# A gated linear attention feeding a PReLU network: first score products issued earlier, half-block products paired, later loads without the zero rows

## The chip, the cores and the metric

The kernel runs on one core of one Trainium2 chip. A core has a matrix engine (PE, with its weight loads shown apart as PEld), a vector engine (DVE), a scalar engine (ACT), a general engine (POOL), an engine that only issues transfers (SP), and 16 DMA engines that all queues share. Each engine works through its own instructions in order. The metric is the device time in microseconds (us); lower is better.

## The reference

Two stages are computed in float32. The first is a recurrence over 768 time steps for 4 batches and 8 heads of width 48; the second is a two-layer network with a PReLU between its layers.

```python
def _attn_ref(q, k, v, f_logit):          # (4, 8, 768, 48)
    f = 1.0 / (1.0 + np.exp(-f_logit))
    state = np.zeros((B, H, D, D))
    for t in range(S):
        state = f[:, :, t, :, None] * state + np.einsum('bhd,bhe->bhde', k[:, :, t], v[:, :, t])
        y[:, :, t] = np.einsum('bhd,bhde->bhe', q[:, :, t], state)
def _moe_ref(x, w_in, w_out, alpha):      # x: (3072, 384), d_ff 2048
    h = x @ w_in
    g = np.maximum(h, 0.0) + alpha * np.minimum(h, 0.0)
    return g @ w_out
```

## The kernel before

**Steps.** The sequence is cut into chunks of 128 time steps, and two batches (`U = 2`) are taken together, which gives 12 steps. The first two steps are the first chunk (`c == 0`) of either pair of batches; the very first one is `bp == 0, c == 0`. A step has four parts, each a generator that is advanced by the letters of a schedule string: `prepare` (letters P and Q), `carry` (O), `attend` (S) and `network` (n). While the network of one step runs, the attention of the next step and the preparation of the one after it are woven in. The order on PE, DVE and ACT is exactly the order of these letters (four strings in `first`, then `usual`); SP and POOL get their order from the framework, which also places the waits.

**Attention.** Within a chunk the scores are built from blocks of 32 (`DB`), 16 and 4 time steps. `prepare` loads `f`, `q`, `k` laid out as 128 rows (two heads of 48 rows, each followed by 16 rows of zeros), takes the sigmoid of `f` on ACT, and forms running products of `f` on DVE. From these come scaled copies of `q` and `k`: `qd` (short distances), `k4` and `us`, `k16` and `q16` (the later half of a block of 32 against its earlier half, for the first chunk only), `kh` and `q3`, `ks`. In `attend`, PE makes the products `raw` (L518: `k` times `qd`) and `qu` (L533: `k4` times `us`) for `u = 0` and then `u = 1`; DVE picks entries of them into `ad` by copies under a mask (L524, L555). ACT copies `ad` into the score matrix `A` (L561), PE multiplies it by the values (`py`, L572), ACT copies `py` to `y` (L581). In `carry`, PE makes `off` (L442 from `kh` and `q3`; L452 from `k16` and `q16`), the transposes `pk` (L469) and the state update `pd` (L482); ACT copies them out (L456 to `ad`, L460 to `A`, L472 to `ksn`, L498 to `vs`).

**Network.** For the first step `xt` (L590) turns `y` into `xT` on PE; later steps do it by DMA. Then 8 groups of `ph` (L614, 12 recorded matmuls each) with a ReLU on ACT (L619) and a combination on DVE (L622), and `po` (L638).

**Weights.** `w_in` and `w_out` each come in 8 pieces. A piece is loaded by SP into one of 4 `raw` buffers; two ACT passes (L197, L199) and three DVE passes (L205, L211, L218) decode it; POOL issues a DMA that adds its last part (L225; for the very first piece DVE adds it, L223). Letters a and b are the ACT halves for `w_in` and `w_out`, w and v the DVE halves. A `w_in` piece holds just what one `ph` group needs.

**PSUM.** `psa` has two buffers of two banks ("pair"), taken in turn by `off`, `pk`, `raw`, `qu`, `pd`, `py`; `psn` has four single banks ("bank") for `xt`, `ph`, `po`. `qd`, `ad` and `A` exist once, and so do the loaded `f`, `q`, `k`.

**Loads.** For the first step SP issues `f`, `q`, `k` and `v`; for all later steps POOL does, in its own order among the weight additions (L264, L274).

Of the kernel before, what the change touches and what calls it, by code (L numbers as in the profile page):

```python
# [8 lines left out]
F32 = mybir.dt.float32  # L9
# [22 lines left out]
def kernel(  # L32
# [63 lines left out]
    def bank(name):  # L96
        return psn.tile([128, 512], F32, tag="net", name=name)

    om = const.tile([128, NF], F32, tag="om", name="om")
    w_in_sb = const.tile([128, NK, DF], F32, tag="w_in", name="w_in_sb")  # L100
    w_out_sb = const.tile([128, NF, DM], F32, tag="w_out", name="w_out_sb")
# [43 lines left out]


    A = const.tile([128, U, H, C], F32, tag="A", name="A")
    nc.gpsimd.memset(A, 0.0)
    vs = []
    for bp in range(B // U):  # L150
# [105 lines left out]
    def prepare(bp, c, x):  # L256
# [2 lines left out]
        b0 = U * bp  # L259
        loads = nc.gpsimd if bp or c else nc.sync  # L260

        def load(name, src, bufs=2):
            t = work.tile([128, W], F32, tag=name, name=f"{name}_{i}", bufs=bufs)
            loads.dma_start(out=t.rearrange("p (u x) -> p u x", u=U),  # L264
                              in_=src[b0:b0 + U, c].rearrange("u p h t -> p u (h t)"))
            return t

        f = quads(load("f", fT, 1))
        q = load("q", qT, 1)
        k = x["k"] = load("k", kT, 1)  # L270

        for cc in range(NC2):
            t_, _ = halves(cc)
            loads.dma_start(out=vs[bp][t_, cc, :, 0:DM], in_=v[b0:b0 + U, c, t_].rearrange("u t d -> t u d"))  # L274


        nc.scalar.activation(f, f, AF.Sigmoid)
        nc.scalar.copy(kr[:, :, 2:3], f[:, :, 3:4])
        qdv = [qd[:, :, QO[d]:QO[d] + NB * (4 - d)].rearrange("p g (i r) -> p g i r", r=4 - d) for d in range(4)]
        nc.scalar.copy(qd[:, :, 0:DB], q.rearrange("p (g t) -> p g t", t=DB))  # L280
# [11 lines left out]
        nc.vector.tensor_tensor(fq, f[:, :, 0:1].rearrange(by32, i=NB), kr[:, :, 0:1].rearrange(by32, i=NB), ALU.mult)  # L292
        lagged(3)
        yield

# [129 lines left out]
                        in_=kt[32 * a:32 * (a + 1), 0:W].rearrange("p (g b x) -> p g b x", b=NJ, x=32)[:, :, b, 0:n])  # L427
        yield

    def carry(bp, c, x):  # L430

        i = f"{bp}_{c}"
        q3, ks, kh, f64 = (x[n] for n in ("q3", "ks", "kh", "f64"))
        off = pair(f"off_{i}")
        for u in range(U):
            for hp in range(HP):
                for cc in range(NC2):
                    g = (u * HP + hp) * NC2 + cc
                    o = (u * HP + hp) * DB
                    for par in range(2):  # L440
                        r_ = rows(par)
                        nc.tensor.matmul(off[CH * cc:CH * cc + DB, par, o:o + DB],  # L442
                                         lhsT=kh[r_, g], rhs=q3[r_, g, 2], start=True, stop=True)
        if not c:
            for u in range(U):
                for hp in range(HP):
                    for j in range(NJ):
                        g = (u * HP + hp) * NJ + j
                        o = U * HP * DB + (u * HP + hp) * 16
                        for par in range(2):  # L450
                            r_ = rows(par)
                            nc.tensor.matmul(off[DB * j:DB * (j + 1), par, o:o + 16], lhsT=x["k16"][r_, g],  # L452
                                             rhs=x["q16"][r_, g], start=True, stop=True)
            for u in range(U):
                o = U * HP * DB + u * HP * 16
                nc.scalar.copy(ad[:, u, :, :, 16:DB], off[:, :, o:o + HP * 16].rearrange("p r (h t) -> p r h t", h=HP))  # L456
        for cc in range(NC2):
            s_ = slice(CH * cc, CH * cc + DB)
            for par in range(2):
                nc.scalar.copy(A[s_, :, par * HP:(par + 1) * HP, CH * cc + DB:CH * (cc + 1)],  # L460
                               off[s_, par, 0:U * HP * DB].rearrange("p (u h t) -> p u h t", u=U, h=HP))


        if not c:
            pk = pair(f"pk_{i}")
            for u in range(U):
                for hp in range(HP):
                    a = (u * HP + hp) * NC2
                    nc.tensor.transpose(pk[:, u, hp * 128:(hp + 1) * 128], ks[:, a:a + 2].rearrange("p c s t -> p (c s t)"), ident)  # L469
            ksn = x["ksn"] = work.tile([128, U, HP * 128], F32, tag="ksn", name=f"ksn_{i}", bufs=1)  # L470
            for u in range(U):
                nc.scalar.copy(ksn[:, u], pk[:, u])  # L472
        yield
        pd = pair(f"pd_{i}")
        ksn = x["ksn"]
        for u in range(U):
            for hp in range(HP):
                for cc in range(NC2):
                    for par in range(2):
                        o = (u * HP + hp) * D  # L480
                        s_ = halves(cc)[0]
                        nc.tensor.matmul(pd[rows(par), cc, o:o + D],  # L482
                                         lhsT=ksn[s_, u, hp * 128 + 64 * par:hp * 128 + 64 * par + D],
                                         rhs=vs[bp][s_, cc, u, (2 * hp + par) * D:(2 * hp + par + 1) * D], start=True, stop=True)

        def moved(cc):

            of, to = halves(cc)[1], halves(1 - cc)[1]
            was, then = (vs[bp][p, a, :, 0:DM].rearrange("p u (h e) -> p u h e", e=D)
                         for p, a in ((of, cc), (to, 1 - cc)))  # L490
            if c or cc:
                nc.vector.tensor_tensor(then, was, f64[of].unsqueeze(3).broadcast_to((D, U, H, D)), ALU.mult)
            for par in range(2):
                now = pd[rows(par), cc, 0:U * HP * D].rearrange("p (u h e) -> p u h e", u=U, e=D)
                if c or cc:
                    nc.vector.tensor_tensor(then[:, :, par:H:2], then[:, :, par:H:2], now, ALU.add)
                else:
                    nc.scalar.copy(then[:, :, par:H:2], now)  # L498

        x["moved"] = moved  # L500
        moved(0)
        yield

    def attend(bp, c, x):

        i = f"{bp}_{c}"
        k, k4, us = (x[n] for n in ("k", "k4", "us"))


        QL, QS = (UW, UW) if c else (VW, C)  # L510
        for u in range(U):
            raw = pair(f"raw{u}_{i}")
            for hp in range(HP):
                for j in range(NJ):
                    g = (u * HP + hp) * NJ + j
                    for par in range(2):
                        r_ = rows(par)
                        nc.tensor.matmul(raw[DB * j:DB * (j + 1), par, hp * C:hp * C + QW],  # L518
                                         lhsT=k[r_, g * DB:(g + 1) * DB], rhs=qd[r_, g], start=True, stop=True)
            adu = ad[:, u].rearrange("p r h (i t) -> p (r h) i t", t=4)  # L520
            rv = raw.rearrange("p r (h x) -> p (r h) x", h=HP)
            for d in range(4):
# [5 lines left out]
            for hp in range(HP):  # L528
                for j in range(NJ):
                    g = (u * HP + hp) * NJ + j  # L530
                    for par in range(2):
                        r_ = rows(par)
                        nc.tensor.matmul(qu[DB * j:DB * (j + 1), par, hp * QS + 4:hp * QS + QL],  # L533
                                         lhsT=k4[r_, g * DB:(g + 1) * DB], rhs=us[r_, g, 4:QL], start=True, stop=True)
            if c:
                for m in range(1, NB):
                    lo = UO[m] + (4 if m == 1 else 0)
                    n = DB - 4 * m
                    nc.vector.copy_predicated(  # L539
                        ad[:, u, :, :, 4 * m:DB],  # L540
                        mquad[:, lo:lo + n].bitcast(I32).unsqueeze(1).unsqueeze(1).broadcast_to((128, 2, HP, n)),
                        qu[:, :, 0:HP * UW].rearrange("p r (h x) -> p r h x", h=HP)[:, :, :, lo:lo + n])
            else:
                qv = qu.rearrange("p r (h x) -> p (r h) x", h=HP)
                adh = ad[:, u].rearrange("p r h (a t) -> p (r h) a t", a=2)
                for m in range(1, NQ):
                    n = 4 * (NQ - m)
                    lo = 4 if m == 1 else VO[m]
                    hi = lo + (DB - 4 if m == 1 else 2 * n)
                    to, of, by = ad[:, u].rearrange("p r h t -> p (r h) t")[:, :, 4:DB], qv[:, :, lo:hi], mhalf[:, lo:hi]  # L550
                    by = by.bitcast(I32).unsqueeze(1).broadcast_to((128, H, hi - lo))
                    if m > 1:
                        to = adh[:, :, :, 4 * m:16]
                        of, by = (t.rearrange("p h (a t) -> p h a t", a=2) for t in (of, by))
                    nc.vector.copy_predicated(to, by, of)  # L555
            yield

        for u in range(U):
            for j in range(NJ):
# [46 lines left out]
    def network(bp, c, x):  # L606
# [44 lines left out]

    steps = [(bp, c) for c in range(NC) for bp in range(B // U)]
    first = (
        "P2 a P w P a P a w O P w S a w S Q a O a w S2 Q w S Q S",
        "P a w a P w2 b n2 v O n b2 v S n v n P S b S v b n S v n b v Q b n b n v O v n v Q3 S2 n2 Q2",
        "O n2 S n2 S Q S2 n3 O n Q n Q2 n S2 n Q2 n",
        "n O n2 S n2 S Q n O Q n2 S Q n S n S Q2 S Q n2",
    )
    usual = "O n S n2 S n2 O n Q n Q2 n2 S3 n Q S n Q n Q"
    pieces = {key: part for keys, parts in (("aw", load_weights(w_in_sb, w_in, "w_in")),  # L660
# [75 lines left out]
```

## Time and profile before

| quantity | us |
|---|---|
| time, median of 8 runs (lowest, highest) | 653.5 (651.24, 654.11) |
| the profiled execution's own time | 650.54 |
| its span in the trace | 648.8 |
| PE busy (7580 matmuls) | 608.4, 94% |
| DVE busy | 423.8, 65% |
| ACT busy | 254.9, 39% |
| POOL busy | 67.6, 10% |

The page gives for each engine its busy time and, in 40 equal slices of 16.2 us, the busy share of each slice in tenths. The chain of work that ended last is followed back from the last instruction; "issue" in it is time for which the profile shows no wait. The timeline merges equal instructions that follow one another: start, length from the first to the last, engine, source line, operation, output and inputs, count, and in brackets the idle time before the first with what ended it. Line numbers are those of the kernel before.

### The profile page before, as it was taken

What the parts mean: (1) busy time and instruction counts of PE and PEld (TensorE: products, weight loads), DVE (VectorE), ACT (ScalarE), POOL (GpSimd) and SP (SyncE); (2) the same over time, 40 slices, a digit from 0 to 9 for tenths busy, and PEclk for the clock granted to TensorE, in tenths of its full rate; (3) what the DMA queues carried; (4) which work ended last, traced back from release to release, by engine and by line L of the source; (5) the groups of instructions that cost most, each with busy time, mean ns of one, the idle gap of its engine ahead of it and who ended that gap; (6) DMA issues with size and microseconds to landing.
All of it is one profiled execution on the core that took longest, in us unless ns stands there. A gap on an engine that the chain in (4) does not pass through costs nothing.

```text
span 648.8 us, 17589 instructions
## 1 busy us (share of the span) xinstructions
PE 608.4 (94%) x7580; PEld 451.5 (70%) x7580; DVE 423.8 (65%) x866; ACT 254.9 (39%) x466; POOL 67.6 (10%) x114
## 2 busy tenths in 40 slices
PE   0449799999999999999999999999999999999997
PEld 0448666866866876876875876876876776786874
DVE  6879798794695785685686686587577476450220
ACT  5676783423343161361361360460361351331210
POOL 9143221000000010010000000000001000000000
PEclk9999899999999999999999999999999999999999
DMA  7998985413223223223213313313213201101000
GB/s 250 279 244 224 288 223 128 112 34 61 59 79 63 70 67 63 69 55 73 72 40 87 74 33 91 74 34 90 68 41 90 52 27 35 42 1 25 24 1 24
DMA packets 73116, 56.22 MB, mean 87 GB/s; under 512 B 47408, under 2 KB 64944, under 8 KB 73040
## 3 DMA queue, kind: packets, MB, share of 16 engines
q0 software_dynamic: 10112, 27.53, 16.0%
q1 hardware_dynamic: 57536, 25.37, 15.4%
q10 hardware_dynamic: 5392, 2.21, 1.6%
q8 instruction: 60, 0.98, 0.6%
q14 instruction: 16, 0.13, 0.1%
HBM read 36.21 MB, written 4.72 MB: 63 GB/s over the span
## 4 chain that ended last, share of the span: by engine, by line
PE 93%; DVE 2%; issue 2%; ACT 2%; DMA 1%; DVEq 0%; ACTq 0%
PE ph L614 40%; PE po L638 39%; PE raw L518 3%; PE py L572 3%; PE qu L533 3%; PE pd L482 2%; PE off L442 1%; PE xt L590 1%; DMA f<-in_fT 1%; ACT A L561 0%; PE pk L469 0%; PE off L452 0%; ACT us L312 0%; DVE ad L524 0%; DVE us L319 0%
## 5 line engine op out<-in xcount | busy, mean ns | idle before, releaser
L614 PE MATMUL ph<-xT,w_in_sb 128*128 128x256 f32 x1152 | 262.2, 385 | 2.6 <-issue 2.6
L638 PE MATMUL po<-w_out_sb,g 128*128 128x384 f32 x768 | 252.9, 488 | 0.0
L614 PEld LDWEIGHTS ph<-xT,w_in_sb 128*128 128x128 f32 x1152 | 216.5, 191 | 35.7 <-issue 6.2
L638 PEld LDWEIGHTS po<-w_out_sb,g 128*128 128x128 f32 x768 | 144.9, 190 | 96.8
L622 DVE SCALAR_TENSOR_TENSOR g<-neg,om,ph 128x256 f32<-128x256 f32 x192 | 83.3, 477 | 163.3 <-ACT neg L619 163.2
L619 ACT ACTIVATE neg<-ph 128x512 f32<-128x512 f32 x96 | 57.4, 601 | 166.3 <-PE ph L614 156.7
L632 ACT COPY o<-po 128x384 f32<-128x384 f32 x24 | 11.5, 478 | 145.6 <-PE po L638 131.7
L524 DVE COPY_PREDICATED ad<-mraw,raw 128x256 f32<-128x256 int32 (+1 forms) x96 | 42.4, 441 | 5.8 <-PE raw L518 3.3
L539 DVE COPY_PREDICATED ad<-mquad,qu 128x224 f32<-128x224 int32 (+6 forms) x140 | 41.9, 299 | 6.2
L561 ACT COPY A<-ad 32x256 f32<-32x256 f32 x96 | 38.4, 400 | 2.2 <-DVE ad L539 0.9
L328 DVE TENSOR_TENSOR us<-us,fs 128x768 f32<-128x768 f32 (+5 forms) x60 | 37.2, 620 | 0.3
L312 ACT COPY us<-qd 128x256 f32<-128x256 f32 x48 | 30.2, 666 | 9.8 <-DVE qd L285 9.7
L264 POOL DMA_DIRECT2D k<-in_kT x11 | 8.3, 759 | 233.8 <-PE raw L518 207.1
L285 DVE TENSOR_TENSOR qd<-qd,f 128x768 f32<-128x768 f32 (+2 forms) x36 | 27.2, 755 | 8.1 <-ACT qd L280 8.0
L572 PEld LDWEIGHTS py<-A,vs 128*64 128x64 f32 x768 | 25.0, 145 | 10.3 <-ACT A L561 8.1
L415 ACT COPY A<-q 48x512 f32<-48x512 f32 x44 | 27.1, 616 | 9.3 <-DVE f L410 4.6
L572 PE MATMUL py<-A,vs 128*64 128x64 f32 x768 | 26.9, 231 | 3.9 <-ACT A L561 3.9
L518 PE MATMUL raw<-qd,k 48*32 48x80 f32 x1536 | 23.8, 243 | 6.6 <-issue 5.2
L518 PEld LDWEIGHTS raw<-qd,k 48*32 48x32 f32 x1536 | 18.7, 109 | 15.0 <-issue 14.3
L442 PE MATMUL off<-q,kh 48*32 48x32 f32 x768 | 9.5, 199 | 18.4 <-DVE q L366 18.4
L581 ACT COPY y<-py 128x512 f32<-128x512 f32 x24 | 12.9, 589 | 35.2 <-PE py L572 35.2
L533 PE MATMUL qu<-us,k 48*32 48x112 f32 (+1 forms) x1536 | 25.5, 259 | 0.0
(85 smaller groups left out, 441.0 us busy)
## 6 DMA issues: line engine op xcount, KB each, us to landing
w_out_raw<-in_w_out SPq DMA_DIRECT2D x8, 767.8 KB, 6.6
w_in_raw<-in_w_in SPq DMA_DIRECT2D x8, 767.2 KB, 7.1
f<-in_fT POOLq DMA_DIRECT2D x11, 512.0 KB, 4.0
q<-in_qT POOLq DMA_DIRECT2D x11, 512.0 KB, 4.1
k<-in_kT POOLq DMA_DIRECT2D x11, 512.0 KB, 4.3
out<-o SPq DMA_DIRECT2D x24, 192.0 KB, 2.1
vs<-in_v POOLq DMA_DIRECT2D x22, 192.0 KB, 3.5
w_out_sb<-w_out_lead POOLq DMA_DIRECT2D x8, 384.0 KB, 5.2
```

The lines of the kernel that those rows point to most:

```text
L312: nc.scalar.copy(q4[:, :, :, r], qdv[r][:, :, :, 0])
L328: nc.vector.tensor_tensor(us[:, :, UO[m]:UO[m] + 4 * n].rearrange("p g (i r) -> p g i r", r=4), us[:, :, skip:skip + 4 * n].rearrange("p g ...
L518: nc.tensor.matmul(raw[DB * j:DB * (j + 1), par, hp * C:hp * C + QW], lhsT=k[r_, g * DB:(g + 1) * DB], rhs=qd[r_, g], start=True, stop=True)
L524: nc.vector.copy_predicated(adu[:, :, :, d:4], mraw[:, d, :, d:4].bitcast(I32).unsqueeze(1).broadcast_to((128, H, NB, n)), rv[:, :, QO[d]: ...
L533: nc.tensor.matmul(qu[DB * j:DB * (j + 1), par, hp * QS + 4:hp * QS + QL], lhsT=k4[r_, g * DB:(g + 1) * DB], rhs=us[r_, g, 4:QL], start=Tr ...
L539: nc.vector.copy_predicated(ad[:, u, :, :, 4 * m:DB], mquad[:, lo:lo + n].bitcast(I32).unsqueeze(1).unsqueeze(1).broadcast_to((128, 2, HP, ...
L561: nc.scalar.copy(A[s_, u, :, s_], ad[s_, u].rearrange("p r h t -> p (r h) t"))
L572: nc.tensor.matmul(py[64 * par:64 * par + 64, u, o:o + CH], lhsT=vs[bp][:, cc, u, hd * D:hd * D + 64], rhs=A[:, u, par * HP + hp, CH * cc: ...
L614: nc.tensor.matmul(ph[:, j * T:(j + 1) * T], lhsT=w_in_sb[:, kt, (f + j) * 128:(f + j + 1) * 128], rhs=xT[:, kt], start=(kt == 0), stop=(k ...
L619: nc.scalar.activation(neg, phv, AF.Relu, scale=-1.0)
L622: nc.vector.scalar_tensor_tensor(g[:, j], neg[:, j], om[:, f + j:f + j + 1], phv[:, j], ALU.mult, ALU.add)
L638: nc.tensor.matmul(po[u][:, 0:DM], lhsT=gs[f // 2][:, f % 2, u * C:(u + 1) * C], rhs=w_out_sb[:, f], start=(f == 0), stop=(f == NF - 1))
```

## The change

- **Score products.** In the very first step, `prepare` makes the `raw` products of both `u` at the start of its second stage (new function `within`). `attend` then does for that step `first` (mask copies of `raw`, then `qu`) for both `u`, and `second` (mask copies of `qu`) for both; other steps keep their order. As `raw` then holds both pairs, `off`, `pk` and `pd` of this step take two single banks each (`two`).
- **Halves of 32.** In the first chunk the `k16` by `q16` products are made for two neighbouring blocks at once, 64 columns by 32; only the two diagonal quarters are used. There are half as many matmuls; ACT copies the quarters into `ad` with 8 copies of 32 rows instead of 2 of 128.
- **Loads.** Of `f`, `q`, `k`, all steps but the first load only the two times 48 rows that are not zero, with two DMAs in place of one; the tiles are allocated once, so that the zero rows stay from the first load. In the first step `f` comes in two DMAs, one for each batch, with a sigmoid for each.
- **Order.** The four strings in `first` are new.

```diff
+    def two(name, begin):
+        if begin:
+            return [bank(f"{name}{k}") for k in range(2)]
+        t = pair(name)
+        return [t[:, k] for k in range(2)]
...
+    ft, q, k = (const.tile([128, W], F32, tag=n, name=n) for n in ("ft", "q", "k"))
...
-        def load(name, src, bufs=2):
-            t = work.tile([128, W], F32, tag=name, name=f"{name}_{i}", bufs=bufs)
-            loads.dma_start(out=t.rearrange("p (u x) -> p u x", u=U),
-                              in_=src[b0:b0 + U, c].rearrange("u p h t -> p u (h t)"))
-            return t
-        f = quads(load("f", fT, 1))
-        q = load("q", qT, 1)
-        k = x["k"] = load("k", kT, 1)
+        def load(t, src, parts=1):
+            n = U // parts
+            for u in range(0, U, n):
+                for r_ in (rows(0), rows(1)) if bp or c else (slice(0, 128),):
+                    loads.dma_start(out=t[r_].rearrange("p (u x) -> p u x", u=U)[:, u:u + n],
+                                    in_=src[b0 + u:b0 + u + n, c, r_].rearrange("u p h t -> p u (h t)"))
+        parts = 1 if bp or c else U
+        load(ft, fT, parts)
+        load(q, qT)
+        load(k, kT)
...
-        nc.scalar.activation(f, f, AF.Sigmoid)
+        for part in range(parts):
+            fp = f[:, part * W // 4 // parts:(part + 1) * W // 4 // parts]
+            nc.scalar.activation(fp, fp, AF.Sigmoid)
...
         yield
+        if not (bp or c):
+            x["raw"] = [within(i, u, k) for u in range(U)]
...
+    def within(i, u, k):
+        raw = pair(f"raw{u}_{i}")
+        for hp in range(HP):
+            for j in range(NJ):
+                g = (u * HP + hp) * NJ + j
+                for par in range(2):
+                    r_ = rows(par)
+                    nc.tensor.matmul(raw[DB * j:DB * (j + 1), par, hp * C:hp * C + QW],
+                                     lhsT=k[r_, g * DB:(g + 1) * DB], rhs=qd[r_, g], start=True, stop=True)
+        return raw
...
-                    for j in range(NJ):
-                        g = (u * HP + hp) * NJ + j
-                        o = U * HP * DB + (u * HP + hp) * 16
+                    for cc in range(NC2):
+                        g = (u * HP + hp) * NJ + 2 * cc
+                        o = at + (u * HP + hp) * DB
                         for par in range(2):
                             r_ = rows(par)
-                            nc.tensor.matmul(off[DB * j:DB * (j + 1), par, o:o + 16], lhsT=x["k16"][r_, g],
-                                             rhs=x["q16"][r_, g], start=True, stop=True)
-            for u in range(U):
-                o = U * HP * DB + u * HP * 16
-                nc.scalar.copy(ad[:, u, :, :, 16:DB], off[:, :, o:o + HP * 16].rearrange("p r (h t) -> p r h t", h=HP))
+                            nc.tensor.matmul(off[par][CH * cc:CH * (cc + 1), o:o + DB],
+                                             lhsT=x["k16"][r_, g:g + 2].rearrange("p g t -> p (g t)"),
+                                             rhs=x["q16"][r_, g:g + 2].rearrange("p g t -> p (g t)"), start=True, stop=True)
+            for par in range(2):
+                for j in range(NJ):
+                    s_ = slice(DB * j, DB * (j + 1))
+                    o = 16 * (j % 2)
+                    nc.scalar.copy(ad[s_, :, par, :, 16:DB],
+                                   off[par][s_, at:2 * at].rearrange("p (u h t) -> p u h t", u=U, h=HP)[:, :, :, o:o + 16])
...
-            yield
+        if begin:
+            for stage in (first, second):
+                for u in range(U):
+                    stage(u)
+                yield
+        else:
+            for u in range(U):
+                first(u)
+                second(u)
+                yield
...
     first = (
-        "P2 a P w P a P a w O P w S a w S Q a O a w S2 Q w S Q S",
-        "P a w a P w2 b n2 v O n b2 v S n v n P S b S v b n S v n b v Q b n b n v O v n v Q3 S2 n2 Q2",
-        "O n2 S n2 S Q S2 n3 O n Q n Q2 n S2 n Q2 n",
-        "n O n2 S n2 S Q n O Q n2 S Q n S n S Q2 S Q n2",
+        "P2 a P a w P2 a O w2 a O P S w S Q S a2 S w Q a w Q2 S w Q S a",
+        "b w2 n O v n S b n v S b2 v P n2 v S b v n Q b v b n S b v3 O Q n2 Q2 n S n Q S n Q",
+        "n O n2 S n2 S Q S n Q O S n3 S n Q n S n Q",
+        "n P O n2 P S n2 S Q n O Q n2 S Q n S n S Q2 S Q n2",
     )
```

## The prediction

> **What bounds the kernel now.** First the page's slices: they tell where PE has room at all.
>
> ```profile
> PE   0449799999999999999999999999999999999997
> ...
> q8 instruction: 60, 0.98, 0.6%
> ```
>
> PE is full from about 50 us to the end; asked for by stretches, it is busy 100.00 of every 100 us from 200 to 600. A gain can come only from the first 80 us, or from less PE work. So next the chain of waits over 0 to 80 us.
>
> ```profile
> 20.06 1.43 PE off L452 x84
> ...
> 24.09 1.58 issue
> ...
> 29.61 2.59 issue
> ...
> 36.00 1.62 issue
> ...
> 47.17 1.08 ACT y L581 x2
> 48.25 0.14 issue
> 48.39 4.76 PE xt L590 x12
> 53.15 5.18 PE ph L614 x24
> ...
> 70.56 1.05 issue
> ...
> 73.11 2.62 issue
> ```
>
> Two things are to be seen. The network starts when `y` leaves ACT at 48.25, so ACT's queue decides. And PE stands five times (9.46 us) for nothing the profile shows. Third, ACT's timeline, for what kept it:
>
> ```profile
> 21.72 0.41 ACT L456 COPY ad<-off 128x128 f32<-128x128 f32 x2
> 22.02 1.26 ACT L460 COPY A<-off 32x256 f32<-32x256 f32 x4
> ...
> 33.30 1.05 ACT L280 COPY qd<-q 128x1024 f32<-128x1024 f32 x1 [3.68 <-PE raw L518]
> ...
> 38.91 0.96 ACT L498 COPY vs<-pd 48x384 f32<-48x384 f32 x2 [2.79 <-PE pd L482]
> ```
>
> ACT waits for the second `raw` (it still reads the single `qd`) and for `pd`, which stands behind both `raw` and `qu` on PE. Fourth, PE's rate after the last stand, by one-microsecond stretches (clock: the sixth value after the stretch):
>
> ```profile
> 77.00:78.00 1.00, 1.00 (x3) 0.76 (x3) 1.00 (x3) 0.68 (x1) 0.00 (x0) 0.50 0.98 261
> ```
>
> After the 2.62 us stand the granted clock is 0.5 to 0.7 for 4 us: 36 `ph` matmuls take 9.72 us, against 7.78 for three groups at 2.59. That is 1.94 more.
>
> **The five stands.** Counting PE's matmuls in the timeline, they come after matmul 222, 349, 476, 984 and 1111: all 127 apart, or a multiple. A matmul with its weight load is two instructions, so 254 and a wait or two. The instruction queue moved 60 packets of 16.3 KB; at (0.98 + 0.13 MB)/17589 = 63 bytes an instruction, a packet is 259. I read the stands as the fetch of the next packet, started when PE enters the one before. From entry to next entry they took 5.3 (20.4 to 25.67), 6.5, 5.4, 7.6 and 4.1 us, mean 5.8; two runs of 4.9 and 4.6 us (603 to 730 to 857) needed no stand. The Trainium skill's Runtime: NRT & Kernel Launch, Instruction fetch mechanics, has the same blocks of 256, fetched during the block before, and calls the crossing mostly hidden; the 9.46 us speak against "hidden" where small matmuls run.
>
> **The change, part by part.**
>
> *ACT up to `y`.* From 21.72 to 47.17 are 25.45 us, of which 6.97 idle (0.50 + 3.68 + 2.79): 18.5 of work. After it, `raw` runs when DVE's last `qd` is made (10.4) and is done by 14, so the wait of `qd` goes. `pd` stands ahead of `qu`: `ksn` ends near 25.5, `pd` took 0.72 + 1.21, so 27.4, before ACT has converted its `w_in` piece (28.0); that wait goes too. Added: one more conversion pair stands ahead of `y` (2 x 0.9), and 8 `ad` copies for 2. Two copies of 128 elements start 0.15 apart (0.41 less one of 0.26), four of 256 take 0.315 each; I take 0.2, the smaller size being nearer: 1.6 for 0.3, +1.3 (bounds 0.9 to 2.2). The fourth `w_in` piece, for which ACT waited until 26.14, still costs about 0.6 (0 to 0.6). Sum 18.5 + 1.8 + 1.3 + 0.6 = 22.2, `y` at 43.9: **3.2 us earlier** (2.3 to 4.2). What else could be late: DVE's mask copies. By its rows `raw` copies run 25.3 to 29.2, a decode to 30.9, `qu` copies to 31.9 and 32.8; ACT wants them at 32.7 and 38.0. PE's `qu` waits for the freed pairs at 27.2 and 29.2. The fifth and sixth pieces are issued after the DVE pass that frees their buffer, at 25.0 and 30.7, and wanted at 36.2 and 42.0: 11.2 us each, where landing took 7.1 in the median and 14.7 at most.
>
> *Start.* A further SP issue (0.46) puts `q` and `k` behind the second half of `f`; half a sigmoid ends up to 0.5 earlier. DVE's first `qd` waits for ACT's copy at 6.20, `q` lands at 5.94. I take 0 (-0.25 to +0.25).
>
> *PE's own work.* From `ph` on PE is the bound, so fewer matmuls count: 128 of L452 took 1.18 to 1.25; 64 of 32 columns (L442) take 0.69 to 0.76, 64 of 48 (L482) 0.87 to 0.94, and 64 columns may reach the latter: **0.45 us** (0.3 to 0.55). The first step's saving lies under DVE.
>
> *Waits in the second step.* `raw` needs a pair that ACT frees after the same 8 copies: by the rows near 57.1, where PE arrives at 57.5; DVE's copies come just in time for the second `raw`. **Loss 0.3** (0 to 0.8).
>
> *The stands.* The packet limits stay at the same matmul counts, but other work lies there. Order of the changed kernel: raw 128, off 64, k16 64, pk 8, pd 64, qu 128, py 64, xt 12, ph 12, off 64, k16 64, pk 8, ph 12, raw 64, qu 64, ph 12, raw 64. The first four limits fall where PE waits anyway. 603 lies in the second `off` (53.1), 730 in the first `raw` 4.9 later: no stand, as in the run of 4.9. 857 lies in the second `raw`, after 26 raw, 64 qu, 12 ph and 25 raw: 0.35 + 0.65 + 2.6 + 0.35 = 3.95 us later; against the mean of 5.8 a stand of 1.85 (0 to 3.65). To 984 there are 6.4 us: 0 (0 to 1.2). Half clock after it: a 1.05 us stand brought none, the 2.62 one did; I take half of 1.94. TensorE: Matmul & The Clock Gate, section HAM oscillation, tolerates idle gaps up to about 3.4 us; here 2.62 was enough, and by the page the sum would be 1.0 better. So 1.05 + 2.62 + 1.94 = 5.6 before, 1.85 + 1.0 after: **2.8 us gained** (-1.2 to 5.6).
>
> *Later loads.* 384 KB for 512, but two POOL issues (0.74 us each) for one. POOL is busy 6.76 us of 100, PE 100.00: nothing gained, nothing lost; without that cover a late load would cost its lateness. The second step's `v` now stands behind a weight addition on POOL (27 instead of 15.8 us, first read near 74), the third step's `k` ahead of the first `w_out` addition (L225), which waits for DVE about as long: 0.
>
> *`w_out`.* PE comes to `po` some 8 us sooner. Before, the last addition was issued at 96.84, landed (5.2) at 102, and was wanted at 98.85 + 0.75 x 10.52 = 106.7. The v letters move forward as well: by DVE's rows the last decode ends near 88.4, lands near 95, wanted at 97 to 100. Cost 0, with 2 us and more to spare; beyond that 1 for 1, so the gain is capped near 9.5.
>
> **Sum.** 3.2 + 0.45 + 2.8 - 0.3 = 6.1. The profiled execution took 650.54 (span 648.8), 2.96 under the median; its sum gives 644.4, and carried to the median of 653.5, **647.4**.
>
> **Rivals.**
> 1. *The stands stay as long* (fetches of 7.6 us, cold again): for it, DMA share was 1.03 and 1.07 in the 60s and 70s, and `w_out` is now loaded just then; against it, one crossing in place of two is tight. 3.2 + 0.45 - 0.3 = 3.35: 650.1.
> 2. *No stand at all* (fetches of 4 us, as the 4.1 one): 3.2 + 0.45 + 5.6 - 0.3 = 9: 644.5.
> 3. *The network does not start sooner*: ACT idles or works 3.2 us more ahead of `y`, so only the later parts count, 2.95: 650.5. For it: its waits were hardly longer than what is added; against: nothing named above is late by 2 us.
> 4. *Slower*: ACT meets a `w_in` piece that has not landed, and all behind it (`y`) waits. It decides from 11.2 + 6.1 = 17.3 us of landing; at 20 us it gives 656.2. For it one piece took 14.7 with DMA at 98%; against, less is loaded then.
>
> **How the numbers follow.** Likeliest case 0.52 (645.5 to 649.5), rival 1 0.20, 2 0.12, 3 0.09, 4 0.07. What this measurement tells from no change is about 0.2%, 1.3 us. Likeliest, 1, 2 and most of 3 are faster: 0.87; same 0.05; slower 0.08. Range 644.0 to 652.0: from the cap on the gain past rivals 1 and 3, with a microsecond for where the median falls between 651.2 and 654.1.
>
> **What would show it.** Right: `raw` near 10 us, no wait of ACT's `qd` on `raw`, `y` from ACT near 44, first `ph` near 50, one stand near 62, `po` near 78. Wrong: ACT waiting for `w_in` between 34 and 44, PE waiting on `w_out` additions, or stands at counts other than multiples of 127 from 95, which would take the fetch out of the explanation.

## The result, and the profile after

The changed kernel takes 655.73 us in the median of 20 runs (653.12 to 657.68); the kernel before, in 56 runs beside them, 652.46 us. The ratio is 1.005 (95% interval 1.004 to 1.0061): **slower by 3.3 us**. The prediction was 647.4 us, range 644.0 to 652.0, with a chance of 0.08 for slower, and the way in which it got slower was none of its four rivals. The profiled execution took 655.61 us (span 653.8, against 648.8).

The first 50 us go much as predicted, the next 35 less so. Line numbers are now those of the changed kernel: `raw` L455, `qu` L565, `off` L472 and L484, `pd` L518, `xt` L636, `ph` L660, `po` L684. This is PE's timeline after, from the start to `po`:

```profile
10.79 2.40 PE L455 MATMUL raw<-qd,k 48*32 48x80 f32 x128 [10.79 <-DVE qd L300]
...
45.46 5.46 PE L636 MATMUL xt<-y,dense 128*128 128x256 f32 x12 [3.43 <-ACT y L627]
...
63.54 0.49 PE L455 MATMUL raw<-qd,k 48*32 48x80 f32 x26
66.08 0.69 PE L455 MATMUL raw<-qd,k 48*32 48x80 f32 x38 [2.05 <-issue]
...
67.32 12.31 PE L660 MATMUL ph<-xT,w_in_sb 128*128 128x256 f32 x48
```

`raw` runs at 10.79. Of the five stands that the prediction counted one is left in this stretch, after 26 matmuls of the second `raw` of the second step. It ends at 66.08, where the prediction had it near 62, and `po` starts at 83.12 for 78; before, it started at 85.29. ACT's timeline shows the rest of the opening, the new copies among it:

```profile
22.40 2.13 ACT L491 COPY ad<-off 32x128 f32<-32x128 f32 x8 [1.45 <-PE off L484]
...
32.38 1.04 ACT L295 COPY qd<-q 128x1024 f32<-128x1024 f32 x1
...
44.24 1.07 ACT L627 COPY y<-py 128x512 f32<-128x512 f32 x2
```

`qd` no longer waits for `raw`, and `y` starts to leave ACT at 44.24, 2.93 us earlier than before. At the second `raw` of the fourth step PE is 3.3 us ahead of the kernel before (171.10 against 174.40, with the same PE work done). Five microseconds later the loss begins. PE's timeline from there:

```profile
171.10 0.94 PE L455 MATMUL raw<-qd,k 48*32 48x80 f32 x64
...
175.66 0.28 PE L518 MATMUL pd<-vs,ksn 64*48 64x48 f32 x2
180.66 2.04 PE L518 MATMUL pd<-vs,ksn 64*48 64x48 f32 x62 [4.72 <-DMA ksn<-kt]
182.63 7.81 PE L660 MATMUL ph<-xT,w_in_sb 128*128 128x256 f32 x24
190.27 10.48 PE L684 MATMUL po<-w_out_sb,g 128*128 128x384 f32 x32
200.69 2.08 PE L618 MATMUL py<-A,vs 128*64 128x64 f32 x64
```

`pd` makes two matmuls and then waits 4.72 us for `ksn`. Before, the same stretch, `pd` to `py`, ran without a wait, as PE's timeline before shows:

```profile
178.87 0.94 PE L482 MATMUL pd<-vs,ksn 64*48 64x48 f32 x64
...
195.43 2.09 PE L572 MATMUL py<-A,vs 128*64 128x64 f32 x64
```

That is 16.56 us from start to start. Now it takes 25.03. The 8.5 us more are 4.72 of wait and 3.7 of slower work: `pd` and the 24 `ph` behind it run at a reduced clock, as the busy times by stretches show (the sixth value after the stretch is the granted clock):

```profile
175.00:180.00 5.00, 0.95 (x6) 0.47 (x4) 4.79 (x13) 2.29 (x4) 0.98 (x2) 1.00 0.74 126
180.00:185.00 5.00, 4.33 (x68) 3.73 (x69) 4.50 (x8) 0.80 (x2) 0.00 (x0) 0.56 0.02 3
185.00:190.00 5.00, 5.00 (x19) 4.19 (x18) 1.05 (x3) 0.60 (x1) 0.00 (x0) 0.76 0.00 0
```

3.3 ahead less 8.5 is 5.2 behind, and the span is 5.0 longer. The medians differ by 3.3 only, since the profiled execution of the kernel before (650.54) is 1.9 us under its median and that of the changed kernel is at its own. Why `ksn` was late shows on two other queues. `ks` is transposed to `kt` by DVE (L437), and SP then issues sixteen transfers that carry `kt` to `ksn` (L442). In the kernel before SP issued them early:

```profile
155.43 12.23 SPq L425 DMA_DIRECT2D ksn<-kt  x16
```

The last was issued at 167.66, which with the median 2.0 us to landing made `ksn` complete near 169.7, 9.2 us ahead of `pd`. DVE's timeline after:

```profile
158.71 0.87 DVE L668 SCALAR_TENSOR_TENSOR g<-neg,om,ph 128x256 f32<-128x256 f32 x2 [12.42 <-ACT neg L665]
...
164.82 0.87 DVE L668 SCALAR_TENSOR_TENSOR g<-neg,om,ph 128x256 f32<-128x256 f32 x2 [1.27 <-ACT neg L665]
165.61 1.24 DVE L437 STREAM_TRANSPOSE kt<-ks 128x1024 f32<-128x1024 f32 x1
```

and SP's:

```profile
166.92 11.69 SPq L442 DMA_DIRECT2D ksn<-kt  x16
```

The new fourth string makes the last two stages of the step's own `prepare` by its letters P, behind one and then three groups of the network (`n P O n2 P`); the old strings had made them with the letter Q at the end of the third string. DVE works in order, so with these stages still to do it stands 12.42 us until the first `ph` group has come through ACT, and the transpose waits for the third. It starts at 165.61, 12.2 us later than before (153.44), and the last transfer lands at 180.6, when PE has been waiting for 4.7 us.

### The profile page after: what moved, and what is told of

Its sections match the earlier page's. It is cut to its first block, busy times and chain, and to the rows that moved or that the text cites. A ratio compares the mean times of both kernels' runs of the same rounds, so it can differ in the third digit from the quotient of the medians.

```text
span 653.8 us, 17427 instructions
## 1 busy us (share of the span) xinstructions
PE 613.4 (94%) x7452; PEld 454.8 (70%) x7452; DVE 423.4 (65%) x866; ACT 259.0 (40%) x479; POOL 81.5 (12%) x147
## 3 DMA queue, kind: packets, MB, share of 16 engines
HBM read 31.88 MB, written 4.72 MB: 56 GB/s over the span
## 4 chain that ended last, share of the span: by engine, by line
PE 87%; SPq 1%; DMA 1%; issue 0%; DVE 0%; ACT 0%; ACTq 0%
PE po L684 38%; PE ph L660 38%; PE py L618 3%; PE qu L565 3%; PE raw L455 3%; PE pd L518 2%; SPq L442 1%; PE off L472 1%; DMA ksn<-kt 1%; DVE kt L437 0%; DVE g L668 0%; ACT neg L665 0%; ACT o L678 0%; ACTq L665 0%
## 5 line engine op out<-in xcount | busy, mean ns | idle before, releaser
L660 PE MATMUL ph<-xT,w_in_sb 128*128 128x256 f32 x1152 | 265.1, 387 | 0.0
L684 PE MATMUL po<-w_out_sb,g 128*128 128x384 f32 x768 | 252.6, 487 | 0.0
L660 PEld LDWEIGHTS ph<-xT,w_in_sb 128*128 128x128 f32 x1152 | 218.3, 193 | 34.1 <-issue 3.4
L684 PEld LDWEIGHTS po<-w_out_sb,g 128*128 128x128 f32 x768 | 145.0, 190 | 97.0
L276 POOL DMA_DIRECT2D k<-in_kT x22 | 12.8, 588 | 242.0 <-PE raw L455 242.0
L455 PE MATMUL raw<-qd,k 48*32 48x80 f32 x1536 | 22.9, 243 | 12.8 <-DVE qd L300 10.8
L300 DVE TENSOR_TENSOR qd<-qd,ft 128x768 f32<-128x768 f32 (+2 forms) x36 | 27.3, 758 | 9.3 <-ACT qd L295 9.3
L455 PEld LDWEIGHTS raw<-qd,k 48*32 48x32 f32 x1536 | 18.3, 109 | 20.3 <-ACT us L329 10.8
L565 PE MATMUL qu<-us,k 48*32 48x112 f32 (+1 forms) x1536 | 25.2, 259 | 0.3 <-ACT ksn L508 0.2
L532 DVE TENSOR_TENSOR vs<-vs,pd 48x384 f32<-48x384 f32 x40 | 22.1, 553 | 2.0 <-PE pd L518 0.5
```

Of the source, the lines that this page charges most:

```text
L660: nc.tensor.matmul(ph[:, j * T:(j + 1) * T], lhsT=w_in_sb[:, kt, (f + j) * 128:(f + j + 1) * 128], rhs=xT[:, kt], start=(kt == 0), stop=(k ...
L684: nc.tensor.matmul(po[u][:, 0:DM], lhsT=gs[f // 2][:, f % 2, u * C:(u + 1) * C], rhs=w_out_sb[:, f], start=(f == 0), stop=(f == NF - 1))
```

## The experiments

All ratios are to the kernel before, from runs on the same chip. Kernels go by short names (e1, e2 and so on), which the text gives where each is introduced. A trace shows one execution, and it can lie some way from its kernel's median: e10's (643.45 us) is the lowest of six with a median of 647.02, e2's (653.86) the lowest of six of which the others took 658.16 to 659.08, e14's (650.13) among the highest of eleven with a median of 647.84.

**The fourth step.** Four kernels take the new third and fourth strings apart from the rest. The first (e1) is the changed kernel with the old two:

```diff
-        "n O n2 S n2 S Q S n Q O S n3 S n Q n S n Q",
-        "n P O n2 P S n2 S Q n O Q n2 S Q n S n S Q2 S Q n2",
+        "O n2 S n2 S Q S2 n3 O n Q n Q2 n S2 n Q2 n",
+        "n O n2 S n2 S Q n O Q n2 S Q n S n S Q2 S Q n2",
```

> The changed kernel with the third and fourth schedule strings of the kernel before. Theory (the loss is the pd of the fourth step, which waits for the ksn transfers that the new strings issue 11 us later: a wait of 4.72, then pd 1.1 and 24 ph 2.4 slower): the wait goes, PE stands at that place as before, and the 3.3 us that were won by 110 us are kept: ratio to the kernel before 0.995 (0.993 to 0.997). Rival (the split loads of f, q, k make the ksn transfers land late, whatever the order): the wait stays, ratio 1.003 to 1.006.

Measured 0.9927 (0.99 to 0.9953), 646.65 us. SP issues the transfers from 151.04 to 162.24, and `pd` at 174.44 does not wait. That is a little better than expected: the 3.3 us had been read against the profiled execution of the kernel before, which lies under its median. The second (e2) is the reverse, the kernel before with only these two new strings:

> The kernel before with only the third and fourth schedule strings of the change. Theory (the order alone makes the wait): pd of the fourth step waits about 5 us for ksn, PE is at half clock after it, 8 us lost: ratio 1.0125 (1.009 to 1.015). Rival (the loads do it): no wait, ratio 0.999 to 1.001.

Measured 1.0093 (1.0064 to 1.0122), 658.26 us: as expected, and slower than the changed kernel itself. PE's timeline of this kernel has the same lines (`pd` is L482 here):

```profile
174.54 0.28 PE L482 MATMUL pd<-vs,ksn 64*48 64x48 f32 x2
179.81 1.95 PE L482 MATMUL pd<-vs,ksn 64*48 64x48 f32 x62 [4.99 <-DMA ksn<-kt]
```

The third (e5) leaves the strings as they are and moves one letter, the second O of the fourth string, behind two more `ph` groups, so that the reader comes later:

```diff
-        "n P O n2 P S n2 S Q n O Q n2 S Q n S n S Q2 S Q n2",
+        "n P O n2 P S n2 S Q n Q n2 O S Q n S n S Q2 S Q n2",
```

> The changed kernel with one letter moved: in the fourth string the second O (pd) stands behind two more groups of ph. The transposes and the ksn transfers stay as late as in the changed kernel. Theory (pd only came too early for them: the last landed at 180.53, two groups of ph take 5.4 us from 175.66): no wait of pd over 0.5 us, ratio 0.995 (0.993 to 0.997). Rival (the late end of the preparation costs by itself, so the wait only moves on to what needs the state, py or later groups): 1.000 to 1.005.

Measured 0.9929 (0.9907 to 0.9951), 646.96 us. The transpose and the transfers are where the changed kernel has them (165.33, and 166.64 to 177.62); only `pd` moved, to 180.56, about one microsecond after the last landing. PE's timeline of it:

```profile
172.60 8.04 PE L660 MATMUL ph<-xT,w_in_sb 128*128 128x256 f32 x36
180.56 0.94 PE L518 MATMUL pd<-vs,ksn 64*48 64x48 f32 x64
```

The fourth (e14) moves the maker instead: the two stages are made at the end of the third string again (`Q2` twice for `Q`), before the network's next step begins, with the old fourth string.

```diff
-        "n O n2 S n2 S Q S n Q O S n3 S n Q n S n Q",
-        "n P O n2 P S n2 S Q n O Q n2 S Q n S n S Q2 S Q n2",
+        "n O n2 S n2 S Q S n Q O S n3 S n Q2 n S n Q2",
+        "n O n2 S n2 S Q n O Q n2 S Q n S n S Q2 S Q n2",
```

> The changed kernel with the last two stages of the fourth step's prepare back at the end of the third string (Q2 twice for Q) and the fourth string of the kernel before; the third string is otherwise the changed one. This moves the maker of ksn early, where e5_pd_two_groups_later moved its reader late. Theory: kt is transposed before 160 us, the sixteen ksn transfers are issued by 172, pd does not wait on them, and the ratio is 0.993 (0.991 to 0.995), the same as e1 and e5. Rival: the earlier transpose and its transfers hold up something else there (the output's stores on SP's queue, y's way through DVE); then 0.996 or more.

Measured 0.9933 (0.991 to 0.9956). The transpose is at 152.54, fourteen of the transfers are issued by 164.12, the last two behind a store of the output by 166.53, and `pd` does not wait. Either end of the dependency mended by itself brings the whole 8 us back, so the rest of the change, taken together, is not what is slower.

**The halves of 32.** The next (e4) is the e1 kernel with the old products of single blocks and the two copies of 128 rows:

```diff
-                    for cc in range(NC2):
-                        g = (u * HP + hp) * NJ + 2 * cc
+                    for j in range(NJ):
+                        g = (u * HP + hp) * NJ + j
...
             for par in range(2):
-                for j in range(NJ):
-                    s_ = slice(DB * j, DB * (j + 1))
...
+                o = U * HP * DB
...
```

> The first experiment without the paired halves: the products of k16 and q16 are made block by block again, and two ACT copies of 128 rows in place of eight of 32. Theory (in the first step the eight copies took 2.13 us of ACT's full queue ahead of y, two took 0.41; PE saved only 0.1 us in the second step): y leaves ACT about 1.7 us sooner, the network starts as much earlier: 1.2 us (0.5 to 2) faster than the first experiment, ratio 0.993. Rival (PE's saving is worth more than ACT's copies): 0.3 us or more slower than the first experiment.

Measured 0.9945 (0.9924 to 0.9967), against e1's 0.9927: not faster; the intervals overlap. It was expected to be 1.2 us faster. The trace shows two effects that work against each other. From the first `raw` to `xt` the e4 kernel needs 33.06 us (11.19 to 44.25), e1 34.64: the eight `ad` copies do cost 1.7 us on ACT (2.14 against 0.43). But the 64 more matmuls in each of the two steps are one more packet of PE's instructions, and there are three stands in place of e1's one of 1.72 us. PE's timeline of e4:

```profile
53.94 0.77 PE L483 MATMUL off<-us 48*32 48x16 f32 x69 [0.64 <-issue]
...
59.45 0.41 PE L455 MATMUL raw<-qd,k 48*32 48x80 f32 x21 [0.50 <-issue]
...
66.02 0.73 PE L455 MATMUL raw<-qd,k 48*32 48x80 f32 x35 [2.27 <-issue]
67.62 11.61 PE L656 MATMUL ph<-xT,w_in_sb 128*128 128x256 f32 x48
```

3.4 us of stands, and a `ph` of 48 that takes 11.61 us where 10.63 is the full rate (e1). The 59 matmuls ahead of the first of these stands are where the prediction's rule (limits at matmul 95 + 127k) puts 730: 672 lie ahead of L483, so after 58.

**The packets.** Two kernels on top of e5 move the limits. The first (e6) makes the 64 matmuls of `raw` for `u = 0` twice, where PE waits for DVE anyway:

```diff
-            x["raw"] = [within(i, u, k) for u in range(U)]
+            x["raw"] = [within(i, u, k, 2 - u) for u in range(U)]
...
-    def within(i, u, k):
+    def within(i, u, k, times=1):
...
-        for hp in range(HP):
+        for hp in [hp for _ in range(times) for hp in range(HP)]:
```

> The kernel of e5_pd_two_groups_later with the 64 first-score matmuls of block 0 made twice in the opening (the same values, into the same place), where PE waits 5.6 us for DVE afterwards anyway. That moves every later limit of the instruction packets 64 matmuls earlier in the work. My theory (a packet's fetch takes about 5.9 us from the entry into the one before): the stand of 2.2 us after 26 of the second raw of step 2 goes; in its place stands lie inside the two qu: about 37 matmuls into the first qu, 0.7 us (0 to 1.5), and about 24 into the second qu, 1.8 us (1.0 to 2.8); time within 0.3% of e5's (ratio to the kernel before 0.990 to 0.996). Rival: what makes PE stand belongs to the place, not to the count (a semaphore or a buffer that the trace does not name); then it stays after 26 of the second raw, some 2.2 us.

Measured 0.998 (0.9966 to 0.9995), 651.11 us: slower than e5, outside what was expected. The place is right and the length is not. PE's timeline:

```profile
64.08 0.92 PE L455 MATMUL raw<-qd,k 48*32 48x80 f32 x64
64.96 0.39 PE L565 MATMUL qu<-us,k 48*32 48x52 f32 x25
68.67 0.81 PE L565 MATMUL qu<-us,k 48*32 48x52 f32 x39 [3.32 <-issue]
69.41 13.38 PE L660 MATMUL ph<-xT,w_in_sb 128*128 128x256 f32 x48
```

The stand has left the second `raw` and stands 25 matmuls into the second `qu`, where the count puts it; the rival, that it belongs to the place, falls. At the limit in the first `qu` there was none, for 0.7 us expected, and here it is 3.32 us for 1.8. From the 37th matmul of the first `qu` (near 61.0) to the resumption at 68.67 are 7.7 us, against a mean of 5.9 in the expectation, and the `ph` behind it lose 2.75 us to the clock.

The second kernel (e9) also gives the stretch between the limits more work, one more `ph` group between the two `raw`:

```diff
-        "b w2 n O v n S b n v S b2 v P n2 v S b v n Q b v b n S b v3 O Q n2 Q2 n S n Q S n Q",
+        "b w2 n O v n S b n v n S b2 v P n v S b v n Q b v b n S b v3 O Q n2 Q2 n S n Q S n Q",
```

> The kernel of e6_raw_twice with one letter of the second string moved: two ph groups, not one, lie between the first raw and qu of step 2 and the second. By the packet counts the limits then fall about 37 into the first qu (5.1 us after the one before, stand 0.7 us, 0 to 1.5) and about 12 into the second qu (6.5 us after the one before: no stand). My theory: stands of 0.7 us in all, no half clock after them, and 3 us (2 to 4) faster than e5: ratio 0.988 (0.985 to 0.991). Rival: the stands follow the place, or the fetch simply takes longer when more other work lies between; then there is one of about 2 us in the second raw or qu still and the ratio stays at 0.993. Second rival: the second qu comes 2.6 us later and DVE's decode of it holds up py; then py waits and the ratio is 0.992 or more although the stands are gone.

Measured 0.9899 (0.9876 to 0.9921), 645.62 us, beside 645.51 us of its variant with whole loads (below) the fastest here. PE's timeline:

```profile
54.42 0.31 PE L484 MATMUL off<-us 48*64 48x32 f32 x5 [0.39 <-issue]
...
67.33 0.70 PE L565 MATMUL qu<-us,k 48*32 48x52 f32 x51 [0.72 <-issue]
67.97 8.04 PE L660 MATMUL ph<-xT,w_in_sb 128*128 128x256 f32 x36
```

The stands of the second step are 1.1 us in all, at the counts again (59 of L484, 13 of the second `qu`, where none was expected), and the `ph` behind run at full rate (8.04 for 36). A stand of 3.86 us in the first step, after 85 of `qu`, lies where `py` waited for ACT in e5. From `raw` to the second step's `py` this execution is 2.8 us shorter than e5's (79.96 against 82.72), of which 0.69 goes again: it reaches the fourth step's `pd` so early that it waits for `ksn` there.

The traces also hold the packets themselves. Asked for in windows of 0.05 us, the DMA view shows one packet of the instruction queue 2.2 to 3.1 us ahead of the end of each of the 37 stands at a limit that lie in the first 80 us of the fourteen traces. Before, the packets come at 22.60, 29.85, 35.25, 69.35 and 73.50 for stands that end at 25.67, 32.20, 37.62, 71.61 and 75.73; in the changed kernel at 63.80 for 66.08, in e6 at 66.15 for 68.67, in e9 at 64.85 for 67.33. That is what would be seen if PE waits there for its next instructions.

**The first two strings.** The next (e7) is the e1 kernel with the old first two strings as well; only the early `raw`, the halves and the loads are left of the change:

> The kernel of e1_old_strings34 with the first two strings of the kernel before as well, so that of the change only the early raw, the halves and the loads are left, without any new order. My theory: the wait of ACT's qd on raw (3.7 us) goes, but pd stands behind more of the other work again, so y leaves ACT only about 1.5 us earlier than before (46.5 to 48 minus the start of the run's own offset, against 47.2), and by the packet counts two stands are left in step 2, about 1.5 us in the ph between the two raw and about 2 us in the second qu; ratio 0.996 (0.992 to 1.000). Rival A: the order of the first two strings brings nothing, all of the gain is in the early raw and the halves; then 0.993 like e1. Rival B: without its order the early raw only delays the rest; then 1.000 or more.

Measured 0.9932 (0.9911 to 0.9954), the same as e1: rival A, and the theory falls. From `raw` to the start of `y` on ACT this kernel needs 33.30 us (10.07 to 43.37), the changed kernel 33.45. So the new order of the opening brings nothing that shows; the intervals leave some 2 us either way. As the halves (e4) and the loads (e12) bring nothing that shows either, the gain is put down to the early `raw`, by elimination: no run has it alone. The stands were counted wrongly in this expectation. With its order limit 857 falls behind the first matmul of the second `raw` and 984 exactly behind the second `qu`, 127 matmuls and about 1.8 us later; there is one stand, there:

```profile
72.15 10.61 PE L660 MATMUL ph<-xT,w_in_sb 128*128 128x256 f32 x36 [3.72 <-issue]
```

1.8 + 3.7 = 5.5 us for this fetch, and 2.6 us lost to the clock in the 36 `ph`.

**The loads.** The next (e3) is the changed kernel with whole loads of 128 rows again in all steps:

```diff
-                for r_ in (rows(0), rows(1)) if bp or c else (slice(0, 128),):
+                for r_ in (slice(0, 128),):
```

> The changed kernel with its later loads whole again: one transfer of 128 rows (512 KB) in place of two of 48 rows each (384 KB). My theory: these loads cost and gain nothing, since PE reads each of them many microseconds after it has landed; the ratio to the kernel before stays at the changed kernel's 1.005 (1.003 to 1.007), and the wait of the fourth step's pd for the last ksn transfer stays 4.7 us (4.2 to 5.2). Rival: the two POOL issues or their smaller packets get in the way of the sixteen ksn transfers, so that the wait is partly theirs; then it falls by a microsecond or more, and the ratio to 1.003 or less. Second rival: the smaller loads help; then the ratio rises to 1.007 or more.

Measured 1.0024 (1.0006 to 1.0043), below the expected range. The wait on `ksn` is still 4.92 us, so the transfers are not held up by the loads. The profiled execution had a stand of only 0.78 us, which raised the question whether the two loads lengthen the fetch. Three more kernels ask that: the same edit on e5 (e10), the same on e9 (e11), and the split loads alone on the kernel before (e12).

> The kernel of e5_pd_two_groups_later (no wait on ksn) with the later loads whole again, 128 rows (512 KB) in one transfer. In e3_full_loads the same edit on the changed kernel left the wait on ksn as it was (4.92 us), yet the stand in the second raw of step 2 was 0.78 us for 2.05 and TensorE kept full clock behind it, and the time was some 1.7 us less. Theory: the two loads of 192 KB get in the way of the instruction packet's fetch, so here too the stand falls from 2.2 us to about 1, the 48 ph behind it from 12.2 us to below 11, and the ratio to 0.989 to 0.991, against e5's 0.993. Rival: one profile's stand is chance, the loads do nothing; then the ratio is 0.9925 to 0.9935 and the stand lies anywhere between 0.5 and 2.5 us.

Measured 0.9927 (0.99 to 0.9954) against e5's 0.9929, as the rival had it, in spite of a profiled execution with a stand of 0.75 us.

> The kernel of e9_no_stand with the later loads whole again. There the stands that are left are short (0.39 and 0.72 us) and no half clock follows them, so there is little for the loads to gain through the fetch. Theory that the loads act through the fetch alone: within 0.15% of e9 (ratio 0.989 to 0.991, at most 0.7 us better), the fastest of all. Rival that the whole loads are better for another reason: 1.5 us faster than e9, ratio 0.988 or less. Rival that they cost: 0.992 or more.

Measured 0.9901 (0.9877 to 0.9925) against e9's 0.9899.

```diff
+    held = {n: const.tile([128, W], F32, tag=n, name=n) for n in ("f", "q", "k")}
...
-            t = work.tile([128, W], F32, tag=name, name=f"{name}_{i}", bufs=bufs)
-            loads.dma_start(out=t.rearrange("p (u x) -> p u x", u=U),
-                              in_=src[b0:b0 + U, c].rearrange("u p h t -> p u (h t)"))
+            t = held[name]
+            for r_ in (rows(0), rows(1)) if bp or c else (slice(0, 128),):
+                loads.dma_start(out=t[r_].rearrange("p (u x) -> p u x", u=U),
+                                in_=src[b0:b0 + U, c, r_].rearrange("u p h t -> p u (h t)"))
```

> The kernel before with one part of the change alone: f, q and k held in fixed tiles and their later loads made as two transfers of 48 rows each (384 KB for 512), without the zero rows. Theory of the prediction: nothing, 1.000 (0.998 to 1.002). Theory from e3_full_loads: the two transfers lengthen the stands of step 2, by 1 to 2.5 us: ratio 1.0015 to 1.004. Rival: less is loaded, so the fetches are faster and the stands shorter: 0.998 or less.

Measured 1.0012 (0.9994 to 1.003), an interval that holds both 1.000 and the lower end of the second theory. Of the four pairs two show no difference (e5 and e10, e9 and e11: 0.0002 each), and in two the split loads are slower, by 0.0026 (the changed kernel against e3, with intervals that overlap from 1.004 to 1.0043) and by 0.0012 (e12). That they cost about a microsecond is neither shown nor excluded; that they gain is not seen. A stand is 0.75 us in one execution (e10) and 2.2 in another of nearly the same kernel (e5); why is not settled.

## Why the prediction was wrong, by its own steps

- **The step that failed: "A gain can come only from the first 80 us."** It is true of gains, and the prediction went on as if it were true of losses: its sum has no term for the new third and fourth strings, although the diff moves P letters there, and "PE 100.00 of every 100" was read as room to spare on all else. In place of nothing the runs showed a wait of 4.72 us there, and 8.5 us with the slower work behind it. The two moved stages carry a DVE transpose and sixteen SP issues, with PE as their reader. The trace of before had all that was needed. These rows of DVE's timeline before are the transpose and the `g` of the third group behind which it was moved:

```profile
153.44 1.25 DVE L420 STREAM_TRANSPOSE kt<-ks 128x1024 f32<-128x1024 f32 x1
...
168.05 0.87 DVE L622 SCALAR_TENSOR_TENSOR g<-neg,om,ph 128x256 f32<-128x256 f32 x2 [1.77 <-ACT neg L619]
```

  A transpose at 168.84 ends at 170.1; sixteen issues of 0.76 and 2.0 us to landing give 184.3, against `pd` at 178.87 (an earlier arrival moves both). That is a wait of some 5.4 us, an estimate; 4.72 was measured, and the clock behind it came on top.
- **ACT up to `y`, 3.2 us earlier:** 2.93 in the profile. The `ad` copies took 2.13 us for the 1.6 taken (bounds 0.9 to 2.2). But its cause was half wrong: e7 shows that the wait of `vs` on `pd`, which the new order was to remove, needs no new order, since with `raw` out of the way `pd` is done early in either.
- **Start, 0:** not told apart; it is inside the 2.93. Of these only 2.3 reach the first `ph` (50.71 against 52.98), since `xt` took 5.46 for 4.76.
- **Halves on PE, 0.45:** 0.11 (1.14 for 64, against 1.25 for 128). It was the 64 columns that cost: in the same view after, 64 matmuls of 32 columns by 32 (L472) take 0.76. What the halves do bring is a packet of instructions less (e4).
- **Waits in the second step, 0.3:** 0.18, `qu` on ACT.
- **Stands, gain 2.8:** the one predicted, after matmul 857, came there, 2.05 us for 1.85. The size was luck: the work between the limits took 4.6 us for 3.95, and from limit to resumption 6.6 went by for 5.8. The clock behind it was mis-sized: half of 1.94 was taken, 1.68 was measured (12.31 for 10.63). And 1.94 itself was too much: 36 `ph` at full rate span 8.04 in the same view, not 7.78, so 9.72 had lost 1.68 before as well. 5.35 before less 3.73 after is 1.6 gained. Sum of the opening: 2.3 + 0.1 + 1.6 - 0.2 = 3.8; 3.3 were there at the fourth step. The five stands are not all of them: the chain before has a sixth, 1.21 us from 34.07, after matmul 456 and so at no limit. The trace has a semaphore event of 1.56 us on PE's weight loads there (33.7 to 35.3), no such event at the five, and no packet at the distance that these have; it is a wait of `pd` whose releaser the profile does not name.
- **Later loads, 0 and `w_out`, 0:** no PE wait on either shows up to `py` of the second step; for the loads a cost of about a microsecond stays possible (e3, e12).

Without the moved stages the total would have lain inside the range: e1, e5 and e14 are 4.4 to 4.8 us faster than before (0.9927 to 0.9933), where 6.1 was forecast; carried to 653.5 us that is 648.7 to 649.1. Shown by runs are the wait, its cause and its price (e1, e2, e5, e14) and the place of the stands (e4, e6, e7, e9). Read from traces, one execution of each kernel, are the half clock's share of the 8.5 us and the length of a fetch; the stretch that took 25.03 us took 24.15 in e2 and 24.25 in e3, with waits of 4.99 and 4.92.

## What to carry to other kernels

Where a schedule is written out by hand, every moved letter has to be followed to its last reader on every queue, also in the stretch where the bounding engine is full: such an engine hides what is early, and pays at once for what is late. For each moved producer, compute when its last transfer lands and hold that against the reader's row in the trace of before; here a slack of 9 us was spent by two stages moved behind three network groups, and a reader moved 5 us later did without it. A wait on a full engine should be priced with the cold clock behind it: here 4.72 us of wait cost 8.5.

## What was not expected of the hardware

**In these runs a stand of about 2 us is enough to halve the clock.** These are the longest stands of the second step in all fourteen traces, with the time that the 36 or 48 `ph` behind them took over their full rate (8.04 and 10.63 us):

| kernel | longest stand, us | lost in the `ph` behind it, us |
|---|---|---|
| e11 | 0.45 | 0 |
| e9 | 0.72 | 0 |
| e10 | 0.75 | 0 |
| e3 | 0.78 | 0 |
| e1 | 1.72 | 0 |
| changed kernel | 2.05 | 1.68 |
| e5 | 2.20 | 1.54 |
| e4 | 2.27 | 0.98 |
| e14 | 2.28 | 1.05 |
| kernel before | 2.62 | 1.68 |
| e12 | 2.87 | 1.68 |
| e6 | 3.32 | 2.75 |
| e2 | 3.45 | 1.68 |
| e7 | 3.72 | 2.57 |

By stretches of 1 us the granted clock falls to 0.50 behind each stand from 2.05 us on, and stays at 1.00 behind those up to 1.72.

The Trainium skill's TensorE: Matmul & The Clock Gate, section HAM oscillation, gives about 3.4 us of idle PE as the gap to avoid. Stands of 2.05 to 3.32 us already cost here, so in these runs 2 us is the number to plan with. With one execution for each, how sharp the edge is stays open, and so does why 2.28 lost less than 2.05 and 3.45 no more. It differs between executions of one kernel: in four of e14's eleven the mean granted clock is 1.000 (643.92 to 646.58 us), in the others 0.994 to 0.997 (646.70 to 650.48).

**The fetch of an instruction packet is not constant.** From the limit at which it is taken to begin to the resumption, it took 5.3 us in e3 and e10, 5.5 in e7, 6.3 in e1, 6.6 in the changed kernel, 6.8 in e5, 7.4 in e9 and 7.7 in e6, where the five before had 4.1 to 7.6. What varies is the time up to the packet, 2.9 (e10) to 5.1 us (e6); from the packet to the resumption it is 2.3 to 2.5 in these eight. What the packet waits for no run shows. A stand can be placed to the matmul, but its length is known to two or three microseconds only. No safe distance between two limits came out: before, runs of 4.9 and 4.6 us needed no stand, and in e9 6.7 us of work still had one. Shifting the limits alone only moved it (e6), more long matmuls between them took it down to 0.72 us (e9).
